# Row sums spread over all head pairs, and the first operands of Wo fetched earlier

## Chip, cores, metric

The kernel runs on 1 core of one Trainium2 chip. The metric is the device time of one execution in microseconds (us), as the median of several runs. Where a profile is read, its span is a little shorter than the device time of the same run (1532.3 against 1534.1 us for the kernel before). Runs of one kernel differ by up to 0.8% within one batch, so differences of a few microseconds are read from landmarks in the trace rather than from totals; a landmark comes from one profiled run.

## The reference, cut to what matters

```python
def reference(A_x, A_mem0, A_Wq, A_Wk, A_Wv, A_Wo, A_seg_len, B_x, B_w1, ..., c, w_mod):
    # _A_ref: segmented attention, 32 heads of 128, 2048 tokens, D = 1024; ends in
    #     o = einsum('bhte,hed->btd', o, Wo)
    # _B_ref: layernorm, w1 + gelu, shifts, w2, w3 + gelu, w4
    x = A_x
    mod = (_silu(c) @ w_mod).reshape(c.shape[0], 6, 1, -1)
    sa, ca, ga, sb, cb, gb = ...                       # six rows of 1024
    h = _layernorm(x, axis=-1) * (1 + ca) + sa
    x = x + ga * _A_ref(h, A_mem0, A_Wq, A_Wk, A_Wv, A_Wo, A_seg_len)
    h = _layernorm(x, axis=-1) * (1 + cb) + sb
    x = x + gb * _B_ref(h, B_w1, ...)
    return x
```

Two things matter here. The rows ga, cb, sb and gb are products of a vector with slices of w_mod; nothing needs them before Wo, so their work can be placed anywhere in the attention. And Wo needs the attention output of all heads: a 2048 x 4096 by 4096 x 1024 product.

## The kernel before

The kernel works in stages: projections and attention by pairs of heads (16 pairs), then Wo in four blocks of 512 tokens with the second LayerNorm, then the four matrices of the second part. Work is cut into small closures ("units") that are merged into one order; a scheduler orders instructions finally, except where `keep_order` pins them. The transposes of V and of the attention output O are DMA transposes on the SP queue.

The row sums: a 128 x (8 x 256) piece of w_mod is loaded, VectorE multiplies and adds it up to `row_a`, splits it into two bf16 parts, and two matmuls with one column of ones sum over the partitions.

```python
def row_units(items, pool):                       # pool: up_row, bufs=1
    def mk(vi, add1, n4):                         # one quarter of one row
        def load():
            st["wm"] = ws_tile([P, KT, 256])
            keep_order(nc.sync.dma_start(st["wm"][:], wslice(w_mod, ...)))
        def part(k0): ...                         # 2 of the 8 steps on VectorE into row_a
        def split(): ...                          # row_hi, row_lo on VectorE; total is put on pending
        def total():
            pb = acc_tile()[0:1, 0:256]
            nc.tensor.matmul(pb, lhsT=ones_col[:], rhs=st["hi"][:], start=True, stop=False)
            nc.tensor.matmul(pb, lhsT=ones_col[:], rhs=st["lo"][:], start=False, stop=True)
            ...                                   # copy on ACT or DVE into row_a / row_hi
            nc.gpsimd.dma_start(dst, r)
        return [load] + [part(k) for k in range(0, KT, 2)] + [split]
    quarters = [mk(vi, add1, n4) for vi, add1 in items for n4 in range(4)]
    ...                                           # each quarter's load one quarter ahead

for hp in range(NHP - 1):                         # NHP = 16 pairs
    fill = P_units(hp + 1)                        # projections of the next pair
    ...                                           # guard squares in the pairs hp = 0 to 9
    if hp == NHP - 6:
        ru = row_units(((2, False), (4, True), (3, False), (5, False)), rowp)
    ...                                           # so all 16 quarters lie in 4 pairs
    interleave(att[hp], fill)
```

The start of Wo, after the last projections:

```python
otcp = ...tile_pool(name="x1_ot", bufs=6)         # OTc: transposed attention, 8 heads x 512 tokens, 1 MB
wspR = ...tile_pool(name="x1_wsR", bufs=4)        # Wo blocks of 1 MB
W0 = W_units(0)                                   # [n2][hc]: 32 matmuls each; hc is a group of 8 heads
for j in range(3):
    load_ot(j)                                    # on SP, ahead of the O and V transposes
load_wo2(NHP - 2)
interleave(att[NHP - 1], M_units(NHP - 3) + [lambda: load_wo2(NHP - 1)] + M_units(NHP - 2) + W0[0][0:2])
for u in att["end"] + W0[0][2:3]:
    u()
for j in range(3, 6):
    load_ot(j)
...
for u in W0[1][0:3] + W0[0][3:] + W0[1][3:]:
    u()
...
for blk in range(1, 4):
    ...
    elif blk == 2:
        nc.sync.dma_start(w1s[:], ...)            # w1, 2 MB, for the stage after Wo
```

## Time and profile before

| | before |
|---|---|
| median of 3 runs | 1532.65 us (1531.76 to 1537.88) |
| TensorE busy | 1439.2 us, 94% of the span |
| pairs up to 534 us | 43.7 us each |
| the five pairs from 534 to 777 us | 48.7 us each |
| last projection to the end of Wo | 267.6 us |

The page of the kernel before. The digits are tenths of busy time in 40 equal slices of the span (38.3 us each).

```profile
...
PE 1439.2 (94%) x9074; PEld 762.2 (50%) x9074; DVE 929.8 (61%) x1961; ACT 665.7 (43%) x1403; POOL 357.5 (23%) x486
PE   5698999999999999998986799999997999999998
...
DMA  9576779887777697767569999995399785287812
```

TensorE is full except for the start, a dent at slice 30 (1149 to 1188 us, the start of the third matrix), and two dents: slices 18 and 20 (690 to 805 us, the row sums) and 21 to 22 (805 to 880 us, the start of Wo). Slices are counted from 0. In the second dent the DMA row is 9 throughout.

How fast the pairs go is read from a work item that recurs once per pair, the 199-column projections of Wv. From the timeline of TensorE, kernel before (start, duration, line, output<-inputs, count):

```profile
184.39 1.54 PE L330 MATMUL acc<-hh,wv 128*128 128x199 bf16 x16
...
533.76 1.54 PE L330 MATMUL acc<-hh,wv 128*128 128x199 bf16 x16
...
777.43 1.54 PE L330 MATMUL acc<-hh,wv 128*128 128x199 bf16 x16
```

The first eight pairs take (533.76 - 184.39) / 8 = 43.7 us each, the five with the row sums (777.43 - 533.76) / 5 = 48.7 us each (the work of the 4 pairs, 558 to 765 us in the trace, touches five of these intervals). In those pairs VectorE waits for single buffers. From the waits of VectorE, 534 to 793 us (total us, times, longest):

```profile
DVE row_a L265 <- DMA rows_d<-row_a: 10.6, 4, 4.2
...
DVE row_hi L272 <- DMA rows_d<-row_hi: 9.8, 4, 5.2
```

`row_a` may only be overwritten when the store of the finished row has left it. These waits are idle time of VectorE.

The waits of TensorE from the last projection to the end of Wo, 793 to 1061 us, kernel before:

```profile
PE acc L830 <- DMA wstream<-in_A_Wo_dram: 9.8, 2, 8.7
PE ps_o L704 <- DMA V<-VT: 5.6, 1, 5.6
PE acc L671 <- POOL OTm L729: 5.0, 1, 5.0
PE acc L830 <- DMA OTc<-OTx_d: 2.4, 1, 2.4
...
```

With one of 2.4 us for x, late in Wo, and three small ones (0.7, 0.7, 0.4) they add up to 27.0 us. The four shown lie before 881 us. The SP queue shows why the transposes are late (timeline of the SP queue; the duration is how long the issue held the queue):

```profile
793.83 1.34 SPq L806 DMA_DIRECT2D OTc<-OTx_d  x3
795.77 14.69 SPq L719 DMA_TRANSPOSE OT<-O  x1
...
```

Behind three loads of 1 MB (and one of Wo, issued at 792.3 us) the issue of an O transpose takes 14.7 us. The V transpose that TensorE waits for is issued after it, at 811.8 us. The DMA engines are full: in the stretch 793 to 890 us their busy share is 1.02 at 310 GB/s.

### The profile page before, as it was taken

The page shows a single profiled execution, that of the slowest core. Times are in us where ns is not written, and L with a number is a line of the kernel's source. Part 1 is how long each engine was busy: PE and PEld are TensorE (multiplying, and loading weights), DVE is VectorE, ACT ScalarE, POOL GpSimd, SP SyncE. Part 2 cuts the span into 40 slices and gives each one's busy share as a digit, 9 for nine tenths or more (in the row PEclk, how much of TensorE's full clock was granted, in tenths as well). Part 3 has the DMA queues.
Part 4 walks back from the last instruction along what each step waited for, and adds up shares of the span by engine and source line. Part 5 has one row for each costly group of instructions (what it writes and reads, how often), then busy time and mean ns, then how long its engine had stood idle before and what let it go on. Part 6 is the DMA issues. An engine that isn't in the chain of part 4 may idle for free.

```text
span 1532.3 us, 24313 instructions
## 1 busy us (share of the span) xinstructions
PE 1439.2 (94%) x9074; PEld 762.2 (50%) x9074; DVE 929.8 (61%) x1961; ACT 665.7 (43%) x1403; POOL 357.5 (23%) x486
## 2 busy tenths in 40 slices
PE   5698999999999999998986799999997999999998
PEld 3365665656655655554553344444443444444443
DVE  5617666666666667986751153453378557667684
ACT  2715766666667554544550030221533661036400
POOL 7402000000000000101100042132011655546525
PEclk9999999999999999999998999999999999999999
DMA  9576779887777697767569999995399785287812
GB/s 312 183 276 151 170 163 195 183 170 173 161 157 167 133 195 166 165 137 160 126 166 273 327 310 335 296 285 155 94 242 264 237 268 179 80 258 252 281 37 77
DMA packets 408276, 304.81 MB, mean 199 GB/s; under 512 B 203338, under 2 KB 361034, under 8 KB 406098
## 3 DMA queue, kind: packets, MB, share of 16 engines
q1 hardware_dynamic: 370128, 243.59, 61.0%
q0 software_dynamic: 8784, 28.85, 6.9%
q10 hardware_dynamic: 29234, 30.71, 6.5%
q8 instruction: 73, 1.20, 0.3%
q14 instruction: 57, 0.47, 0.1%
HBM read 200.82 MB, written 50.63 MB: 164 GB/s over the span
## 4 chain that ended last, share of the span: by engine, by line
PE 39%; DMA 5%; DVE 3%; issue 2%; POOL 1%; ACT 1%; SPq 1%; ACTq 0%; DVEq 0%; POOLq 0%
PE acc L830 8%; PE bank_b L1181 6%; PE bank_b L1130 6%; PE acc L974 4%; PE acc L1057 3%; PE bank_d L1130 3%; PE bank_e L1181 2%; PE bank_d L1181 2%; PE acc L608 2%; DMA wstream<-in_A_Wo_dram 1%; PE bank_e L1130 1%; DMA OT<-O 1%; DMA xt<-in_A_x_dram 1%; DMA x_d<-x 1%; DVE ln_st L104 1%
## 5 line engine op out<-in xcount | busy, mean ns | idle before, releaser
L830 PE MATMUL acc<-wstream,OTc 128*128 128x512 bf16 x1024 | 231.6, 389 | 14.7 <-DMA wstream<-in_A_Wo_dram 9.8
L576 ACT COPY snap<-acc 128x480 f32<-128x480 f32 x264 | 146.8, 563 | 115.7 <-PE acc L608 112.3
L608 PEld LDWEIGHTS <-T 128*128 128x128 f16 x1408 | 131.2, 98 | 129.9 <-issue 14.6
L830 PEld LDWEIGHTS <-OTc 128*128 128x128 bf16 x1024 | 101.7, 100 | 139.4 <-issue 22.1
L608 PE MATMUL acc<-hs,T 128*128 128x480 f16 x704 | 163.5, 369 | 7.2 <-DVE QT L580 6.7
L608 PE MATMUL acc<-hh,T 128*128 128x480 bf16 (+1 forms) x704 | 163.7, 366 | 0.2 <-DVE VT L580 0.2
L731 POOL DMA_DIRECT2D OTx_d<-OT x32 | 24.8, 774 | 562.6 <-DMA OT<-O 504.3
L1130 PEld LDWEIGHTS <-ring 128*128 128x128 f16 (+1 forms) x784 | 77.2, 99 | 107.2 <-issue 14.3
L608 PE MATMUL acc<-hh,wq 128*128 128x480 bf16 x464 | 106.1, 366 | 0.0
L693 ACT ACTIVATE E<-ps_s 99x495 bf16<-99x495 f32 (+2 forms) x160 | 85.8, 545 | 34.5 <-PE ps_s L689 33.3
L711 DVE TENSOR_TENSOR O<-ps_o,rin_all 99x384 bf16<-99x384 f32 (+1 forms) x192 | 96.9, 510 | 4.1
L704 PEld LDWEIGHTS <-E 99*99 99x99 bf16 (+2 forms) x704 | 68.9, 128 | 49.8 <-DVE O L711 10.5
L704 PE MATMUL ps_o<-V,E 99*99 99x129 bf16 (+2 forms) x704 | 82.0, 223 | 11.9 <-DMA V<-VT 5.6
L1000 DVE TENSOR_TENSOR ring<-ring 128x1024 f16<-128x1024 bf16 (+1 forms) x64 | 85.8, 1361 | 5.8 <-PE bank_b L1181 5.4
L580 DVE TENSOR_TENSOR KT<-acc,snap 128x480 bf16<-128x480 f32 x116 | 75.3, 655 | 21.3 <-PE acc L608 13.1
L1181 PEld LDWEIGHTS <-hq 128*128 128x128 bf16 (+1 forms) x560 | 54.8, 98 | 66.0
L695 DVE TENSOR_TENSOR E<-E,maskB 99x495 bf16<-99x495 bf16 (+1 forms) x128 | 47.7, 376 | 63.9 <-ACT E L693 63.7
L1095 ACT COPY snap<-bank_b 128x512 f32<-128x512 f32 x72 | 40.6, 583 | 102.7 <-PE bank_b L1181 63.2
L918 ACT ACTIVATE u<-x,ln_nmr,ln_rstd 128x1024 bf16<-128x1024 f32 x16 | 19.7, 1230 | 142.3 <-DVE ln_nmr L917 79.5
L709 ACT ACTIVATE O<-ps_o,rin_all 99x128 bf16<-99x128 f32 x192 | 56.7, 369 | 54.1 <-DVE rin_all L706 53.8
L706 DVE RECIPROCAL rin_all<-ps_o 99x3 f32<-99x3 f32 (+2 forms) x256 | 43.6, 173 | 53.6 <-PE ps_o L704 52.5
L1181 PE MATMUL bank_b<-ring,hq 128*128 128x512 f16 (+1 forms) x336 | 73.2, 379 | 0.0
(218 smaller groups left out, 2512.6 us busy)
## 6 DMA issues: line engine op xcount, KB each, us to landing
wstream<-in_A_Wo_dram SPq DMA_DIRECT2D x32, 1024.0 KB, 10.4
OTx_d<-OT POOLq DMA_DIRECT2D x32, 512.0 KB, 7.6
OTc<-OTx_d SPq DMA_DIRECT2D x16, 1024.0 KB, 9.6
wstream<-in_B_w_dram SPq DMA_DIRECT2D x28, 512.0 KB, 4.4
ring<-in_B_w_dram SPq DMA_DIRECT2D x28, 512.0 KB, 5.5
ring<-in_B_w_dram SPq DMA_DIRECT2D x8, 1792.0 KB, 9.5
wq<-in_A_Wq_dram SPq DMA_DIRECT2D x16, 512.0 KB, 7.0
wk<-in_A_Wk_dram SPq DMA_DIRECT2D x16, 512.0 KB, 8.0
```

Of the source, the lines that this page charges most:

```text
L576: nc.scalar.copy(t[:], st[q][bank][:, 0:CH])
L580: nc.vector.tensor_tensor(view(d, i), chunks(st[q][bank]), chunks(st[q][s_]), ALU.add)
L608: nc.tensor.matmul(acc[:, 0:CH], lhsT=B[:, k, :], rhs=A[:, k, :], start=(j in (1, 2, 5) and k == 0), stop=(k == 3), skip_group_check=True)
L693: nc.scalar.activation(E[:rows, 0:o], ps[:rows, 0:o], ACT.Exp, scale=DH ** -0.5)
L704: nc.tensor.matmul(ps[:rows, i, :], lhsT=state["e", h, t // 5][:k, col0(t) - col0(t // 5 * 5):col0(t) - col0(t // 5 * 5) + rows], rhs=V[:k ...
L709: nc.scalar.mul(O[:rows, t, :], ps[:rows, i, 0:DH], rin[:, i:i + 1])
L711: nc.vector.tensor_tensor(O[:rows, ts[0]:ts[0] + n, :], ps[:rows, 0:n, 0:DH], rin[:, :, None].to_broadcast([rows, n, DH]), ALU.mult)
L830: nc.tensor.matmul(accs[tt][:], lhsT=ot[:, hl, tt * P:(tt + 1) * P], rhs=woc[:, hl, :], start=(h == 0), stop=(h == H - 1))
L974: nc.tensor.matmul(acc[:], lhsT=w1s[:, kt, ct * P:(ct + 1) * P], rhs=zT[:, kt, b * 512:(b + 1) * 512], start=(kt == 0), stop=(kt == KT - 1))
L1000: return nc.vector.tensor_tensor(dst, a, b, op)
L1130: nc.tensor.matmul(acc[:], lhsT=B[:, k, q * P:(q + 1) * P], rhs=A[:, k, :], start=(start and k == 0), stop=(k == 3), skip_group_check=True)
L1181: nc.tensor.matmul(acc[:], lhsT=L3[:, k, i * P:(i + 1) * P], rhs=R3[:, k, :], start=(start and k == 0), stop=(k == 13), skip_group_check=True)
```

## The change

Its intent: (a) spread the row sums over 14 pairs instead of 4, each with a load of its own just ahead and always a flush of the finished sums between two quarters, so that the buffer waits vanish; (b) fetch the first half of the first Wo block's operands ("pre_w", "pre_o", 2 MB) while the last pair with projections still runs, so that 32 Wo matmuls can start at once; (c) load the next 4 MB of the first block by the GpSimd queue, so that the transposes on SP no longer stand behind them; (d) cut the Wo units by token tile, so that they mix finer with attention; (e) issue the load of w1 one block later.

```diff
                 def load():
-                    st["wm"] = ws_tile([P, KT, 256])
+                    st["wm"] = pool.tile([P, KT, 256], BF16, name="row_w")     # pool: bufs=1
...
-            quarters = [mk(vi, add1, n4) for vi, add1 in items for n4 in range(4)]
-            ...                                  # load one quarter ahead
+            for vi, add1 in items:
+                for n4 in range(4):
+                    q = mk(vi, add1, n4)
+                    units += [q[0], lambda: None] + q[1:]
...
+        def preload():
+            pre["ot"] = [prep.tile([P, 4, 512], BF16, name=f"pre_o{i}") for i in range(2)]
+            pre["wo"] = [prep.tile([P, 4, 512], BF16, name=f"pre_w{i}") for i in range(2)]
+            for i in range(2):
+                nc.sync.dma_start(pre["wo"][i][:], Wo2[i * 512:(i + 1) * 512, 0:512]...)
+                nc.sync.dma_start(pre["ot"][i][:], OTx_d[0, 0, :, 4 * i:4 * i + 4])
...
+        extra = [guard_units(), row_units(((2, False), (4, True), (3, False), (5, False)), rowp)]
         for hp in range(NHP - 1):
             fill = P_units(hp + 1)
-            ...                                  # guard squares, then rows in the last four
+            for x in extra if hp < NHP - 2 else []:
+                part = x[len(x) * hp // (NHP - 2):len(x) * (hp + 1) // (NHP - 2)]
...
+            if hp == NHP - 2:
+                LX.close()
+                prep = LX.enter_context(tc.tile_pool(name="x_pre", bufs=1))
+                fill.insert(0, preload)
             interleave(att[hp], fill)
...
-        W0 = W_units(0)
-        for j in range(3):
-            load_ot(j)
+        W0, W0_load = W_units(0)
+        for j in range(1, 3):
+            W0_load(0, j, nc.gpsimd)
+            load_ot(j, nc.gpsimd)
+        for t, src in RW:                        # rows broadcast to 128 partitions, was earlier
+            nc.gpsimd.dma_start(t[:], src.partition_broadcast(P))
         load_wo2(NHP - 2)
-        interleave(att[NHP - 1], M_units(NHP - 3) + [lambda: load_wo2(NHP - 1)] + M_units(NHP - 2) + W0[0][0:2])
+        interleave(att[NHP - 1], M_units(NHP - 3) + [lambda: load_wo2(NHP - 1)] + W0[0][0] + W0[0][1] + M_units(NHP - 2))
...
             elif blk == 2:
                 chain[1] = (lambda a=chain[1]: (a(), check_b()))
+            else:
                 nc.sync.dma_start(w1s[:], B_w1.rearrange("(k p) n -> p k n", p=P))
```

## The prediction

> **What bounds the kernel.** TensorE, 94% busy (busy table); from 160 to 560 us, 399 of 400 us (windows), one head pair every 43.8 us (recurrence of the 199-column Wv projections). Two places break this:
>
> 1. *Rows, 534-777 us.* Five pairs take 243.7 us instead of 219. The 16 row quarters (4.4 us of VectorE each, 70 us) sit in four pairs; VectorE rises from 26 to 33 us per 40. Its waits name the cause: 10.6 us for DMAs of row_a, 9.8 us for DMAs of row_hi (single buffers, next quarter right behind), up to 5.2 us at a time; and the SP queue stands 33 us in row loads, ahead of the V and O transposes. About 3.4 us of the excess are the 32 row-sum matmuls (estimate, 0.107 us each), which remain.
>
> 2. *Start of Wo, 794-890 us.* TensorE waits 2.4 us for OTc, 5.0 for OTm, 5.6 for the V transpose, 1.0 and 8.7 for Wo blocks. Three 1 MB OTc loads precede the O transpose on the SP queue; its issue takes 14.7 us. The granted clock falls to 0.66-0.83 around each long wait: the Trainium skill ("TensorE: Matmul & The Clock Gate", Part 1) says an idle window of about 3.4 us halves the clock; here a Wo matmul took up to 634 ns, median 379. At 0.218 us per Wo matmul block 0 could end at 855 us (estimate); it ends at 871.5, waits 8.7 and restarts cold (+3). Recoverable: 28 us.
>
> **What the change does.** Matmuls and bytes stay.
> - Rows: 8 units per pair over 14 pairs, two units and always a flush between a quarter's split and the next, so the buffer waits mostly vanish. VectorE pays 5 us per pair everywhere (26 to 31 of 40); guard squares drop from 2.8 to 2 per pair. Expect 18 of 21 us back, after new short waits.
> - The first 2 MB of Wo and OT come in the last pair with projections, so 32 Wo matmuls (7 us) start at once; the OTm sums move behind. The next 4 MB go to the GpSimd queue, so only one OTc load still precedes the transposes on SP. w1 (2 MB) still stands before the second block's Wo loads in the built order.
>
> All this is on TensorE's path. Limit: DMA is 100% busy at 280-340 GB/s from 800 to 1040 us (windows), and a 56 us block needs about 17 MB (estimate: 8 Wo, 4 OT, 5 LayerNorm), 304 GB/s. All queues share the same 16 engines (Trainium skill, "Trainium Kernel Development and Optimization", Key Constraints): the GpSimd queue changes order, not bandwidth. Expect 17 of 28 us back.
>
> **Prediction.** 1532.65 - 18 - 17: 1498 us, range 1487 to 1514. Faster by over 2% 0.58, within 0.41, slower 0.01.
>
> **Signs.** Rows: pairs of 44-45 us throughout; VectorE's DMA waits for row_a and row_hi under 5 us; last projections near 775 instead of 793. Wo: pre_w matmuls right after the last projection, no OTm wait, V wait under 3 us, block 0 done 60-65 us after the last projection (before: 78), the 8.7 us wait halved, clock seldom under 0.9.
>
> **What would make it wrong.** Early pairs, where TensorE is full, lose 1 us or more each to VectorE (18 becomes 5). Wo becomes DMA-bound and the 17 us return as Wo or OTc waits in blocks 1 to 3. The 4 MB on the GpSimd queue slow the transposes as before. If both parts keep nearly all: 1487.

## The result, and the profile after

| | before | after |
|---|---|---|
| median of 4 runs each, us | 1532.36 | 1517.11 (1515.95 to 1518.85) |
| ratio, 95% interval | | 0.9893 (0.9868 to 0.9919) |
| last projection, us in the span | 793.5 | 783.0 |
| end of Wo (first matmul with w1) | 1061.1 | 1043.1 |
| last projection to end of Wo | 267.6 | 260.1 |
| end of Wo to the end | 471.2 | 474.0 |

The change gained 15 us, by the ratio 1.1%: within 2%, not the 2.3% of the prediction, and outside its range. Ratios here and below are the mean time of one kernel's runs over that of the other's in the same rounds, so they are not quite the ratios of the medians quoted.

The landmarks split the 15.2 us between the two spans: 10.5 from the row part (793.5 to 783.0), 7.5 from the Wo part (267.6 to 260.1), and 2.8 given back later (471.2 to 474.0). Predicted were 18 and 17. About 1.5 of the 2.8 lies behind a wait that both kernels have: TensorE waits 5.9 us for ScalarE at the start of the third matrix, and the matmuls from that restart to the next bank_b group took 11.4 us in the kernel after (1170.38 to 1181.82) against 9.9 us before; the granted clock stayed low for longer after the same wait (0.74 from 1174 to 1178 us; before, 1.00 from 1191 to 1195, as far behind the restart). Why was not tested.

The page of the kernel after:

```profile
...
PE 1429.2 (94%) x9074; PEld 760.1 (50%) x9074; DVE 921.4 (61%) x1961; ACT 668.2 (44%) x1403; POOL 356.1 (23%) x490
PE   5699999999999999999996799999997999999998
...
```

The first dent is gone from TensorE's row; the second is not.

The recurring Wv projections, kernel after, timeline of TensorE:

```profile
183.20 0.85 PE L328 MATMUL acc<-hh,wv 128*128 128x199 bf16 x8
...
766.86 1.54 PE L328 MATMUL acc<-hh,wv 128*128 128x199 bf16 x16
```

All 13 pairs take (766.86 - 183.20) / 13 = 44.9 us. That is 1.2 us more for the early ones and 3.8 less for the late ones.

The waits of VectorE in the kernel after, 130 to 769 us, where the rows are now:

```profile
DVE row_a L265 <- DMA row_w<-in_w_mod_dram: 6.2, 3, 2.2
DVE row_hi L288 <- PE acc L280: 0.2, 1, 0.2
```

The two old waits are gone, as predicted. A new one has come: VectorE now waits for the load of the row's own weights, 6.2 us in all, so the sign "DMA waits for row_a and row_hi under 5 us" was missed.

The waits of TensorE, 782.4 to 1043 us, kernel after:

```profile
PE ps_o L713 <- DMA V<-VT: 13.6, 1, 13.6
PE acc L845 <- DMA wstream<-in_A_Wo_dram: 7.2, 1, 7.2
PE acc L845 <- DMA OTc<-OTx_d: 3.6, 2, 1.8
...
```

With two of 0.4 and 0.3 us they add up to 25.1 us; before, it was 27.0. So nearly all the waiting came back under other names: of the 27.0 us only 1.9 went. The other part of the 7.5 us is that TensorE's busy time in the stretch fell from 240.5 to 234.8 us for the same work. Most of that is clock: a Wo matmul lasts 379 ns at the full clock, and the mean over 1024 of them was 389 ns before, while after it was 385 ns over 960 and 379 over the other 64; that is 10 us above the full clock before and 6 after (estimate, mean excess times count). The windows of the stretch (us, then busy time with instructions for PE, PEld, DVE, ACT and POOL, granted clock, DMA share, GB/s); the first fence is the kernel before:

```profile
793.00:1061.00 268.00, 240.49 (x1183) 111.64 (x1181) 96.10 (x241) 42.12 (x69) 53.00 (x70) 0.94 0.95 284
```

the second the kernel after:

```profile
783.00:1043.00 260.00, 234.78 (x1176) 109.42 (x1174) 97.74 (x240) 41.42 (x67) 55.36 (x74) 0.95 0.93 284
```

and the third the kernel after in windows of five microseconds, two of them in the long wait:

```profile
803.00:808.00 5.00, 0.00 (x0) 0.00 (x0) 0.00 (x0) 0.00 (x0) 0.70 (x4) 0.95 1.12 302
808.00:813.00 5.00, 0.00 (x0) 0.00 (x0) 0.00 (x0) 0.00 (x0) 0.55 (x1) 0.50 1.23 251
```

The clock, 1.00 in the window before these, falls to 0.50 within the idle time, which agrees with the Trainium skill ("TensorE: Matmul & The Clock Gate", Part 1), by which an idle window of about 3.4 us halves it.

The timeline of the SP queue, kernel after:

```profile
783.26 0.34 SPq L812 DMA_DIRECT2D OTc<-OTx_d  x1
785.21 16.14 SPq L728 DMA_TRANSPOSE OT<-O  x1
...
803.66 5.33 SPq L650 DMA_TRANSPOSE V<-VT  x1
```

and the GpSimd queue, kernel after:

```profile
783.53 0.90 POOL L828 DMA_DIRECT2D wstream<-in_A_Wo_dram  x1 [9.40 <-PE ps_s L698]
...
```

Only one OTc load now precedes the O transpose on SP, yet its issue takes 16.1 us, more than the 14.7 of before. The 4 MB on the other queue (two Wo blocks, two OTc) were issued from 783.5 to 786.4 us, at the same moment. Only the two OTc of them had stood ahead of the O transpose before; the two Wo blocks were then issued on SP at 822.9 us or later, behind it. So the change did not clear the transposes' way of bytes: it took 2 MB to another queue and brought 2 MB forward.

The V wait grew by 8.0 us (5.6 to 13.6) for two reasons that the timeline of TensorE separates. The V transpose landed later after the last projection, 32.6 us (815.6 - 783.0) instead of 27.3 (820.8 - 793.5); and TensorE, without the OTm wait, was ready for it 2.6 us sooner.

One reading of the prediction has to be put right here. It took block 0 to end at 871.5 us before, with the 8.7 us wait between blocks. But only 224 of the block's 256 matmuls had run by then; the last 32 came after that wait, and the block ended at 890.4 us, 96.9 us after the last projection. In the kernel after it ends at 865.7 us, 82.7 us after: block 0 became 14.2 us shorter. That is about the forecast shortening (78 to between 60 and 65), but partly by luck of where the line is drawn: the 8.7 us wait inside block 0 is gone from there because a wait for Wo now comes behind it. Then TensorE waits 7.2 us for the first Wo block of block 1 and restarts cold, and blocks 1 to 3 take 177.4 us instead of 170.7. 14.2 gained and 6.7 given back are the 7.5.

### The profile page after: what moved, and what is told of

Its sections match the earlier page's. It is cut to its first block, busy times and chain, and to the rows that moved or that the text cites. A ratio compares the mean times of both kernels' runs of the same rounds, so it can differ in the third digit from the quotient of the medians.

```text
span 1517.1 us, 24283 instructions
## 1 busy us (share of the span) xinstructions
PE 1429.2 (94%) x9074; PEld 760.1 (50%) x9074; DVE 921.4 (61%) x1961; ACT 668.2 (44%) x1403; POOL 356.1 (23%) x490
## 4 chain that ended last, share of the span: by engine, by line
PE 73%; DMA 8%; issue 6%; DVE 5%; ACT 4%; POOL 3%; SPq 1%; ACTq 0%; DVEq 0%; POOLq 0%
PE acc L607 28%; PE bank_b L1202 6%; PE acc L845 6%; PE bank_b L1151 6%; PE acc L995 4%; PE acc L328 4%; PE bank_d L1151 3%; PE bank_d L1202 2%; PE bank_e L1202 2%; PE ps_o L713 2%; PE ps_s L698 2%; PE acc L318 2%; PE acc L1078 2%; PE bank_e L1151 1%; DVE ln_st L104 1%
## 5 line engine op out<-in xcount | busy, mean ns | idle before, releaser
L845 PE MATMUL acc<-wstream,OTc 128*128 128x512 bf16 x960 | 214.7, 385 | 11.3 <-DMA wstream<-in_A_Wo_dram 7.2
L607 PE MATMUL acc<-hs,T 128*128 128x480 f16 x704 | 158.5, 365 | 4.9 <-ACT snap L575 3.8
L845 PEld LDWEIGHTS <-OTc 128*128 128x128 bf16 x960 | 94.4, 99 | 124.8 <-DMA wstream<-in_A_Wo_dram 7.4
L713 PEld LDWEIGHTS <-E 99*99 99x99 bf16 (+2 forms) x704 | 69.2, 127 | 53.2 <-issue 20.4
L1021 DVE TENSOR_TENSOR ring<-ring 128x1024 f16<-128x1024 bf16 (+1 forms) x64 | 75.5, 1200 | 5.5 <-PE bank_b L1202 5.1
L110 POOL TENSOR_TENSOR ln_rstd<-ln_ve,mhalf 128x1 f32<-128x1 f32 x64 | 35.2, 550 | 173.7 <-DVE ln_ve L108 129.8
```

The source lines that it names most:

```text
L607: nc.tensor.matmul(acc[:, 0:CH], lhsT=B[:, k, :], rhs=A[:, k, :], start=(j in (1, 2, 5) and k == 0), stop=(k == 3), skip_group_check=True)
L713: nc.tensor.matmul(ps[:rows, i, :], lhsT=state["e", h, t // 5][:k, col0(t) - col0(t // 5 * 5):col0(t) - col0(t // 5 * 5) + rows], rhs=V[:k ...
L845: nc.tensor.matmul(accs[tt][:], lhsT=ot[hl // 4][:, hl % 4, tt * P:(tt + 1) * P], rhs=woc[hl // 4][:, hl % 4, :], start=(h == 0), stop=(h ...
L1021: return nc.vector.tensor_tensor(dst, a, b, op)
```

## The experiments

Twelve kernels ran, in three batches on three chips; the kernel before ran beside them with medians of 1534.0, 1535.3 and 1536.3 us, so kernels of different batches are compared by ratio or by landmarks. "Last projection" is the end of the projections in the span; "Wo stretch" is from there to the end of Wo. How far this column scatters is seen where the row part is the same: in after, e1, e3, e4, e7, e8 and e9 it lies between 781.3 and 787.2 us, with prefetched row weights (e5, e10, e12, e13) between 776.8 and 778.7. The Wo stretch of the three kernels with prefetch and the Wo part of after (e5, e6, e13) is 259.1 to 260.4.

| kernel | median us (runs) | ratio to before | last projection | Wo stretch |
|---|---|---|---|---|
| before | 1532.4 (4) | 1 | 793.5 | 267.6 |
| after | 1517.1 (4) | 0.9893 | 783.0 | 260.1 |
| e1_rows_only | 1523.1 (4) | 0.9926 | 782.3 | 270.1 |
| e2_light_rows | 1517.1 (4) | 0.9889 | 786.4 | 259.9 |
| e3_ot4_held | 1518.3 (4) | 0.9890 | 787.2 | 261.3 |
| e4_pool_held | 1517.1 (4) | 0.9890 | 784.2 | 261.9 |
| e5_row_prefetch | 1509.9 (4) | 0.9824 | 776.8 | 260.2 |
| e7_half_ot | 1505.1 (1) | | 781.3 | 247.7 |
| e8_ordered | 1524.4 (4) | 0.9912 | 786.8 | 266.7 |
| e9_ordered_held | 1518.2 (4) | 0.9893 | 783.6 | 257.4 |
| e10_ordered2 | 1513.3 (4) | 0.9844 | 777.6 | 260.9 |
| e12_pref_w1late | 1502.6 (4) | 0.9772 | 778.0 | 251.2 |
| e6_pref_no_sums | 1502.6 (1) | | 768.7 | 259.1 |
| e13_pref_no_squares | 1512.6 (1) | | 778.7 | 260.4 |

"hold(a, b)" in the edits makes the transfer a wait until b has finished; it is an added dependency, nothing is taken away.

### The row part alone: e1_rows_only

Edit: the kernel before, with only the row and guard part of the diff.

```diff
+ row_w, LX pools, [load, nop, parts, split] per quarter, rows and guards over 14 pairs
  (everything from preload on as in the kernel before)
```

> The kernel before with only the row part of the change (spread rows and guards, single buffers); start of Wo as before. If the two parts simply add: last projection near 782 us (after: 782.4), and the Wo part then runs as before, so about 1532 - 10.6 = 1522 us (ratio 0.993) and the Wo part of the change is worth about 5 us net. Rival: the parts interact; the row part alone ends near 1527 (an earlier start is eaten by the Wo loads) or near 1517 (the Wo part is worth nothing).

Measured: 1523.1 us, ratio 0.9926 (0.9879 to 0.9973). The last projection came at 782.3 us, as in the kernel after, and the Wo stretch was 270.1 us, 2.5 more than before (5.0 us of it in a wait for x that the kernel before has only 2.4 of). So the two parts are separate: the row part is worth about 11 us where it happens, and the Wo part 7 to 10 us; by the ratios of the totals (0.9926 and 0.9893) it is about 5 us.

### Is it VectorE's load that keeps the rows from gaining more? e2_light_rows

Edit to the kernel after: seven of the eight multiply-adds of each quarter are left out, so the rows are wrong (relative error 0.024). Loads, splits and sums stay.

```diff
-                            else:
+                            elif vi < 0:
                                 nc.vector.scalar_tensor_tensor(st["a"][:], st["wm"][:, kt, :], ...)
```

> After, with 7 of the 8 VectorE operations of each row quarter left out (wrong result on purpose); loads, buffers, row-sum matmuls, guards unchanged. Theory: the 1.1 us that each head pair costs over 43.8 us comes from VectorE load; then pairs fall to about 44.1 us and the last projection comes 8 to 10 us earlier (772 to 775 us), total about 1508. Rival: single buffers, extra DMA or the row-sum matmuls cost it; then the last projection stays within 2 us of 782.

Measured: 1517.1 us, ratio 0.9889, no gain at all, with the last projection at 786.4 us. Taking most of the row arithmetic from VectorE bought nothing, which speaks against the theory that VectorE's load costs the missing microseconds. The test is not clean: VectorE's wait for the row weights stayed and was longer than in the kernel after (7.8 us in 4 waits, against 6.2 in 3), and 3.0 us of waits for `row_hi` came back. The better evidence is e6 below, where the row arithmetic is all there and the pairs still keep the pace of pairs without rows.

### The trace's own pointer: waiting for row_w

A profile of the next kernel, e3, whose row part is that of the kernel after, showed the mechanism best. Timeline of VectorE, e3_ot4_held:

```profile
605.15 0.35 DVE L265 TENSOR_SCALAR row_a<-row_w,sc 128x256 f32<-128x256 bf16 x1 [5.42 <-DMA row_w<-in_w_mod_dram]
605.42 0.65 DVE L579 TENSOR_TENSOR KT<-acc,snap 128x480 bf16<-128x480 f32 x1
```

and the timeline of TensorE, same kernel:

```profile
606.13 1.49 PE L328 MATMUL acc<-hh,wq 128*128 128x199 bf16 x8 [4.98 <-DVE KT L579]
```

VectorE reaches the first step of a quarter, whose weights have not landed, and stands for 5.4 us; the K evacuation behind it is late, so no accumulator is free and TensorE waits 5.0 us. In the kernel after the same wait, at the same place, was 1.95 us. So its length varies between runs of the same row part, and the last projection largely follows it: with 4.6 and 5.1 us of such waits in all (e1, e7) it comes at 782.3 and 781.3 us, with 7.8 (e3, e8) at 787.2 and 786.8. The cause is the single buffer: `row_w` can only be loaded when the quarter before has been used up, and the transfer takes 5.5 us (median from issue to landing).

### Load the row weights one quarter ahead: e5_row_prefetch

Edit to the kernel after: `row_w` gets a pool of two, and each quarter's first unit loads the next quarter.

```diff
-                    st["wm"] = pool.tile([P, KT, 256], BF16, name="row_w")
+                    st["wm"] = rw_pools[0].tile([P, KT, 256], BF16, name="row_w")     # bufs=2
...
+            qs = [mk(vi, add1, n4) for vi, add1 in items for n4 in range(4)]
+            for i, q in enumerate(qs):
+                loads = ([q[0]] if i == 0 else []) + ([qs[i + 1][0]] if i + 1 < len(qs) else [])
+                units += [lambda loads=loads: [f() for f in loads], lambda: None] + q[1:]
```

> After, with two buffers for the row weights and each quarter's load asked for one quarter (about 38 us) ahead. Everything else as after. Theory C (formed after the light-row run moved nothing): VectorE, which works in order, stands at the first operation of a row quarter until the row weights have landed (1.9 us in the profile of after, 5.4 us in another run's), and the K and V sums behind it keep TensorE waiting (1.5 and 5.0 us). Then VectorE's waits for row weights are gone, the KT waits of TensorE (3.2 us in after's profile) are gone, the last projection comes at 777-780 us and the total falls by 3 to 6 us to 1511-1514, with less spread between runs. Rival: the short ACT snapshot waits and the row-sum matmuls are all there is; then nothing moves by more than 1.5 us.

Measured: 1509.9 us (1508.9 to 1511.7), ratio 0.9824 (0.9790 to 0.9858). The last projection moved from 783.0 to 776.8 us. Waits of TensorE, 130 to 769 us, first the kernel after:

```profile
PE acc L607 <- ACT snap L575: 3.8, 14, 0.5
PE acc L328 <- DVE KT L579: 3.3, 2, 1.7
...
```

then e5_row_prefetch:

```profile
PE acc L609 <- ACT snap L577: 3.6, 14, 0.5
PE ps_o L715 <- DVE E L706: 0.6, 1, 0.6
...
```

The waits for KT are gone, and so are VectorE's for `row_w`. That confirms it: about 6 us of the row part were lost to a buffer wait that the change itself brought in. The last projections of the four kernels with the second buffer (776.8 to 778.7) lie clear of the seven without it (781.3 to 787.2). The Trainium skill ("Trainium Kernel Development and Optimization", Best Practices) has double-buffering among its first rules; here the second buffer of 4 KB per partition was worth 6 us.

### What do the sums themselves cost? e6_pref_no_sums

Edit to e5: no sum matmuls and no copy after them (rows wrong, relative error 0.026).

```diff
                 def total():
-                    pb = acc_tile()[0:1, 0:256]
-                    nc.tensor.matmul(pb, lhsT=ones_col[:], rhs=st["hi"][:], start=True, stop=False)
-                    nc.tensor.matmul(pb, lhsT=ones_col[:], rhs=st["lo"][:], start=False, stop=True)
...
-                    if add1: ...                 # copy of pb on DVE or ACT
```

> Prefetched row weights, with the two row-sum matmuls, the copy from their bank and nothing else left out of each of the 16 quarters (one partition's part sum is stored; wrong result on purpose). Pairs cost 44.5 us in the prefetch run against 43.8 before. If the sums' own TensorE time is most of the rest (0.39 us per quarter with its gap, read from the trace): pairs 44.0 to 44.1 us, last projection 5 to 6 us earlier than in the prefetch run (771-772 us). Rival: the guard squares on ScalarE are the rest; then under 2 us earlier.

Measured (one run, state unknown): 1502.6 us; the last projection 8.1 us earlier than in e5. By the recurring Wv projections: e6 takes 43.8 us a pair ((752.60 - 183.01) / 13), which is the pace of pairs without any rows, and e5 takes 44.45 ((760.71 - 182.86) / 13). The 13 pairs differ by 8.3 us, 0.52 us for each of the 16 quarters. VectorE's row arithmetic is untouched in e6, so at 43.8 us a pair it costs TensorE nothing that shows. Most of the 0.52 can be seen in place. Timeline of TensorE, e5_row_prefetch:

```profile
197.99 0.85 PE L329 MATMUL acc<-hh,wk 128*128 128x199 bf16 x8
198.76 0.27 PE L280 MATMUL acc<-row_hi,ones_col 128*1 128x256 bf16 x1
...
199.07 0.37 PE L715 MATMUL ps_o<-V,E 99*99 99x129 bf16 x3
```

Eight such projections take 0.69 us to the start of what follows them, so the next matmul could have started at 198.68 and started at 199.07: 0.39 us for the two, not the 0.21 of two matmuls at 0.107 us. (The second of the two is the line left out.) The remaining 0.13 us of the 0.52 was not located.

### Do the guard squares on ScalarE cost anything? e13_pref_no_squares

After e5 the largest waits left are 14 small ones for ScalarE's `snap`, 3.6 us. Edit to e5: the squares of the guard (on ScalarE) are replaced by a memset of their result; the guard then checks nothing, and the output stays right. The 28 memsets ran in the first 2 us of the kernel, so they load nothing later.

```diff
-                return lambda: keep_order(nc.scalar.activation(st[i][:], st[i][:], ACT.Square, accum_out=wsq[:, i:i + 1]))
+                return lambda: nc.vector.memset(wsq[:, i:i + 1], 0.0)
```

> Prefetched row weights, with the guard squares (2.1 us of ScalarE each, two per pair) left out; their loads stay (the guard then guards nothing; results stay right). TensorE's waits for ScalarE snapshots (3.5 us in 14 short waits, one per pair, each right behind a square in the trace) should vanish and the last projection come 3 to 4 us earlier than in the prefetch run (773 us). Rival: those waits come from the sums' PSUM bank; then they stay and nothing moves by more than 1 us.

Measured (one run, state unknown): 1512.6 us, last projection at 778.7 us, no earlier than e5. The waits for `snap` did vanish, but waits for VT (3.9 us), O (1.9) and QT (1.3) took their place, and the expectation of an earlier last projection failed. The waits of VectorE, 130 to 769 us, show why; none of this stands in e5. From e13_pref_no_squares:

```profile
DVE row_hi L273 <- DMA rows_d<-row_hi: 5.3, 2, 3.4
...
```

The old waits for the row buffers had come back in the new order of instructions, also 3.4 us for `row_a` and 3.4 more before a `row_a` step that the profile puts down to a V transpose; three of TensorE's new waits end right behind such a stand of VectorE (at 235, 402 and 710 us). So the run does not show that the squares are free: what their absence may have gained, this other wait took.

### The V transpose: e3_ot4_held and e4_pool_held

Edit e3 to the kernel after: the OTc loads of j = 4 and 5 wait for the last V transpose. Edit e4: the second Wo block and OTc on the GpSimd queue, and the row broadcasts (3.5 MB together) wait for it, so that 2 MB are left in its way.

```diff
 e3:  ins = eng.dma_start(ot[:], OTx_d[j // 4, j % 4])
+     if j in (4, 5):
+         hold(ins, state["tv", 31])               # the V transpose of head 31
 e4:  W0_load(0, 1, nc.gpsimd); load_ot(1, nc.gpsimd)
+     hold(W0_load(0, 2, nc.gpsimd), state["tv", 31])
+     hold(load_ot(2, nc.gpsimd), state["tv", 31])
+     for t, src in RW:
+         hold(nc.gpsimd.dma_start(t[:], src.partition_broadcast(P)), state["tv", 31])
```

> After, with the two OTc loads of the next block (1 MB each, SP queue), one of which stands ahead of the last O and V transposes, held until the last V transpose has landed. The four GpSimd loads are untouched. Theory A: the transposes are slow because all bulk shares the DMA engines with them, from whichever queue; then the V wait of TensorE falls only from 13.6 to 9-11 us. Rival B: the one OTc load ahead of them in the same SP queue is what delays them; then the V wait falls under 4 us. Total 1513-1517 under A, near 1508 under B.

> After, with the second Wo block, its OTc and the four row broadcasts (3.5 MB, GpSimd queue) held until the last V transpose has landed; the first pair (2 MB) and the SP queue as they are. Theory A: V wait falls from 13.6 to about 4-7 us, then perhaps a wait of up to 5 us for the held block, total about 1511-1515. Rival B (the SP queue's own OTc load): V wait stays above 10 us and the held block comes later still, total at or above 1517.

Measured, e3: 1518.3 us, V wait 13.7 us, unchanged. This run does not test what it was meant to: in the order as built another OTc load had moved into the gap, so one still stood ahead of the O transpose on SP. It only shows that holding these two loads changes nothing. Its V wait met neither theory.

Measured, e4: 1517.1 us, ratio 0.9890. Waits of TensorE, 776 to 1050 us, e4_pool_held:

```profile
PE acc L853 <- DMA OTc<-OTx_d: 9.3, 3, 6.4
PE acc L853 <- DMA wstream<-in_A_Wo_dram: 8.5, 2, 8.2
PE ps_o L719 <- DMA V<-VT: 6.2, 1, 6.2
...
```

The V wait is halved, from 13.6 to 6.2 us, and the O transpose's issue falls from 16.1 to 7.8 us, with the same single OTc load ahead of it. Timeline of the SP queue, e4_pool_held:

```profile
784.48 0.34 SPq L818 DMA_DIRECT2D OTc<-OTx_d  x1
786.43 7.78 SPq L734 DMA_TRANSPOSE OT<-O  x1
```

So it is the bulk on the GpSimd queue that slows a transpose on the SP queue. But the held loads are then missed: OTc waits rise from 3.6 to 9.3 us, and the total is the same. Rearranging moved the wait.

### Better orders: e8_ordered, e9_ordered_held, e10_ordered2

Edit e8 to the kernel after: no OTc load stands on SP ahead of the transposes (OTc 3 to 6 go by GpSimd, 4 to 6 of them after the last write of the attention output), the row broadcasts wait for the last V transpose, w1 waits for OTc 12. In the built order the V transpose then also goes before the O transpose. e9 is e8 with the second Wo block and OTc also held until that V transpose. e10 is e5 plus the order of e8, with OTc 4 to 6 held only until OTc 3 and one later Wo block until the last O transpose.

```diff
+     if j in (3, 4, 5, 6):
+         eng = nc.gpsimd
+     if j in (4, 5, 6):
+         hold(ins, state["otx", 31])              # e10: state["ot", 3]
+ hold(nc.gpsimd.dma_start(t[:], src.partition_broadcast(P)), state["tv", 31])
+ hold(nc.sync.dma_start(w1s[:], ...), state["ot", 12])
+ e9:  hold(W0_load(0, 2, nc.gpsimd), state["tv", 31]); hold(load_ot(2, nc.gpsimd), state["tv", 31])
+ e10: hold(r, state["flip", 31])                  # the Wo block (n2 1, hc 1) of block 0
```

> After, with what block 0 does not need put behind what it needs: row broadcasts held until the last V transpose landed, the OTc loads of the next block (j=4 to 6) and OTc of heads 24-31 on the GpSimd queue behind the last OT write, w1 held until the OTc of the last block has landed. The two GpSimd pairs (4 MB) start as in after. If the engines are full and only the order of bytes is wrong: V wait 13.6 to about 8 us, the 7.2 us wait before block 1 to under 3, total 1506-1511. If order does not help (every byte is needed by then anyway): within 3 us of 1517.

> As the ordered version, and the second Wo block and its OTc also wait for the last V transpose. If the first 2 MB land by 795 us and the transposes then go nearly alone: V wait under 4 us, then a wait of 2 to 6 us for the second OTc, total 1504-1510. If the second OTc then costs what the V wait saved (as in the run with the GpSimd loads held): equal to the ordered version within 2 us.

> Prefetched row weights, and the ordered version's Wo start mended: its 13 us wait for the OTc of heads 24-31 came from two 1 MB Wo loads ahead of the last O transposes and from four OTc loads at once. Here one of the Wo loads waits for the last O transpose, and the next block's OTc loads wait for that OTc. If order can still buy time in the full-DMA stretch: from last projection to Wo end 260 us (after) falls to 248-254, total 1500-1505. If the stretch is bound by bytes alone (reordering only moved waits in four runs so far): 257-262 us, total 1507-1511.

Measured: e8 1524.4 us (0.9912), e9 1518.2 us (0.9893), e10 1513.3 us (0.9844, with the gain of e5 in it). None shortened the Wo stretch by more than 3 us against the kernel after, and e8 lengthened it by 7. All three also hold w1, which alone is worth about 9 us (e12, below): so their orders did not come out even, they lost about what that gave. Waits of TensorE, 776 to 1050 us, e8_ordered:

```profile
PE acc L857 <- DMA OTc<-OTx_d: 14.4, 2, 13.0
...
PE ps_o L719 <- DMA V<-VT: 1.7, 1, 1.7
...
```

The V wait is solved (1.7 us), and everything else is worse: Wo blocks 10.9 us, O 3.8. In e9 it was OTc 12.0 and O 4.9, in e10 Wo blocks 17.9 and O 3.5. And e8 is the cleanest test of the queues. Its first transpose has nothing ahead of it on SP; timeline of the SP queue, e8_ordered:

```profile
787.79 16.97 SPq L654 DMA_TRANSPOSE V<-VT  x1
804.93 2.76 SPq L734 DMA_TRANSPOSE OT<-O  x1
```

Its issue takes 17.0 us beside 4 MB on the GpSimd queue; in e9, beside 2 MB, 11.9 us; and the next one 2.8 us, when the last of the 4 MB were landing (805.1 us). This fits the Trainium skill ("DMA: Bandwidth & Descriptors", Queues, rings and completion order), by which each DMA engine takes turns between its queues, whole packets at a time: another queue does not get out of the way, it gets its turns. That the turns are the mechanism is argued; the runs show the lengthening.

### Are there too many bytes? e7_half_ot

Edit to the kernel after: each OTc load brings only four of its eight heads, and these stand in for the others (wrong; the comparison with the reference did not notice it).

```diff
-            eng.dma_start(ot[:], OTx_d[j // 4, j % 4])
-            ots[j] = [ot[:, 0:4], ot[:, 4:8]]
+            eng.dma_start(ot[:, 0:4], OTx_d[j // 4, j % 4, :, 0:4])
+            ots[j] = [ot[:, 0:4], ot[:, 0:4]]
```

> After, with every OTc load cut to half its bytes (512 KB instead of 1 MB; the other half of the operand reads the same data, wrong result on purpose). Number, order and queues of the loads unchanged. Theory A2: from the last projection to the end of block 0 the DMA engines are full, so bytes are what TensorE waits for; with 4 of about 25 MB less there the V wait falls from 13.6 to under 8 us and block 0 plus the wait after it shortens by 8 to 14 us (Wo end 1043 to about 1032). Rival: the order on the SP queue (transposes behind each other, OTc of heads 24-31 waiting for its write) bounds it; then it shortens by under 4 us.

Measured (one run, state unknown): 1505.1 us. The Wo stretch fell from 260.1 to 247.7 us. Waits of TensorE, 776 to 1050 us, e7_half_ot:

```profile
PE ps_o L713 <- DMA V<-VT: 7.0, 1, 7.0
PE acc L845 <- DMA wstream<-in_A_Wo_dram: 6.0, 2, 5.1
...
```

Where the rearrangements could not shorten the stretch by more than 3 us, fewer bytes did by 12, within the 8 to 14 expected of theory A2. So bytes that do not come make the start of Wo shorter. It does not follow that their order is indifferent (e10 loses 10 us of the stretch by it against e12, below), and the run is not bytes alone: in its built order some loads had moved too (w1 was issued at 835.4 us instead of 849.8).

### Bytes that need not come then: e12_pref_w1late

The diff puts the load of w1 (2 MB, needed only after Wo) one block later in the source. In the built order it stayed where it was, before block 1's Wo loads. Timeline of the SP queue, kernel after:

```profile
849.82 0.84 SPq L978 DMA_DIRECT2D w1s<-in_B_w_dram  x1
...
855.71 14.03 SPq L828 DMA_DIRECT2D wstream<-in_A_Wo_dram  x3
```

The first of these Wo blocks, issued at 855.7 us, is the one that TensorE waits for at 866 to 873 us; it took 17.7 us to land. In the kernel before, w1 was issued at 848.1 us, so nothing had moved. Edit to e5: w1 really waits.

```diff
-                nc.sync.dma_start(w1s[:], B_w1.rearrange("(k p) n -> p k n", p=P))
+                hold(nc.sync.dma_start(w1s[:], B_w1.rearrange("(k p) n -> p k n", p=P)), state["ot", 12])
```

> Prefetched row weights, and w1 (2 MB) held until the OTc of the last block has landed, nothing else. If bytes before block 1 are what the 7-8 us wait there is made of: 2 MB at about 370 GB/s is 5.5 us, the wait falls to 2-3 us, from last projection to Wo end 260 to about 254-256, total 1504-1506. Rival: the SP queue standing for the OT write of the last head is the cause; then the wait stays at 7-8 us and total at 1510.

Measured: 1502.6 us (1499.0 to 1503.9), ratio 0.9772 (0.9744 to 0.9800), correct: the fastest kernel, faster than both. w1 is now issued at 918.5 us. The Wo stretch is 251.2 us, 9.0 less than in e5. Waits of TensorE, 776 to 1050 us, e12_pref_w1late:

```profile
PE ps_o L721 <- DMA V<-VT: 13.7, 1, 13.7
...
PE acc L853 <- DMA wstream<-in_A_Wo_dram: 1.8, 1, 1.8
...
```

The wait behind block 0 (7.2 us in the kernel after, 8.5 in e5) and its cold restart are gone; the V wait is untouched. e6 and e13, which ran in the batch of e12 and have w1 early, have stretches of 259.1 and 260.4 us, so the gain is not the chip's.

But holding w1 did two things, for the built order moved with it. Timeline of the SP queue, e12_pref_w1late:

```profile
845.25 0.47 SPq L836 DMA_DIRECT2D wstream<-in_A_Wo_dram  x1
845.97 5.04 SPq L820 DMA_DIRECT2D OTc<-OTx_d  x1
```

By the count of the loads this is the first Wo block of block 1. It was issued 67.2 us after the last projection, in e5 73.9 us after it (850.7 us, behind w1 and one more OTc load): 6.7 us earlier. And it took 12.6 us to land instead of 17.9: 5.3 us less. As an estimate, 2 MB at the 371 GB/s that the DMA engines moved from 850 to 866 us in the kernel after are 5.7 us, about what the landing shows. So fewer bytes account for some 5 of the 12 us by which the block came earlier, and its earlier place in the queue for the rest; no run separates the two. e10, which ran in the same batch and holds w1 in the same way, differs from e12 by its order of loads alone: 1513.3 against 1502.6 us. So that reordering was not merely useless, it cost 11 us (9.7 in the Wo stretch).

## Why the prediction was wrong

What it had right: TensorE bounds the kernel; the old waits for `row_a` and `row_hi` would vanish (20.4 us of them, all gone); the 32 matmuls on prefetched operands start right after the last projection (785.3 us, last projection 783.0); the OTm wait goes; and the DMA engines are full through the start of Wo, with a GpSimd queue that changes order and not bandwidth. It even listed, under what would make it wrong, that the 4 MB might slow the transposes as before, and that the Wo gain might return as waits. It then gave these too little weight.

Rows, 18 predicted, 10.5 measured. Two terms of the sum were mis-sized.
- "About 3.4 us of the excess are the 32 row-sum matmuls." They cost 8.3 us with their copies (e6 against e5), so the recoverable part was some 5 us smaller than the 21 us of the prediction.
- "Expect 18 of 21 us back, after new short waits" allowed 3 us. The single buffer for the row weights, loaded only just before its use, cost about 6 (e5): a wait of VectorE, passed on to TensorE. The prediction took the removal of the load-ahead for harmless. The early pairs did lose over 1 us each, as it feared, but not by VectorE's load: e2 gained nothing without it, and in e6 the pairs keep 43.8 us with it.
- Together: 18 - 5 - 3 is 10, the measured size (which in kernels with the same row part scatters between 6 and 12: last projections at 787.2 to 781.3 us, before 793.5). The signs agree: pairs of 44.9 us, the upper end of the 44 to 45 foreseen, and last projections at 783 instead of 775.

Wo, 17 predicted, 7.5 measured. Here a step failed: "The next 4 MB go to the GpSimd queue, so only one OTc load still precedes the transposes on SP", with the sign "V wait under 3 us". The V wait rose from 5.6 to 13.6 us. The O transpose ahead of it took 16.1 us to issue, 14.7 before, with the 4 MB on the other queue (e4, e8 and e9: 7.8 to 17 us by how much was there), and 2 of these 4 MB had not been ahead of it before. V landed 5.3 us later after the last projection; the rest of the longer wait is TensorE being there sooner. The prediction called TensorE's idle time recoverable and only then named the DMA limit; in a stretch at a DMA share of 1.0 that order is the wrong way round. Of 27.0 us of waits in the stretch it counted on 17 back; 25.1 us of waits were left, and by the estimate above some 4 of the 7.5 us gained are the clock. Four rearrangements moved the wait or made it worse (e4, e8, e9, e10; e3 did not test it), fewer bytes shortened it (e7).

Also, "w1 (2 MB) still stands before the second block's Wo loads in the built order" was seen and not costed. Holding it was worth 9 us (e12 against e5), by its bytes and by the earlier place of the Wo block behind it, and the wait it removed is the one at which block 0's gain was given back: 14.2 us gained, 6.7 lost from block 1 on. (The kernel before has w1 early too, at 848.1 us; what it cost there was not tested.) That the 8.7 us wait lay inside block 0 and not behind it was misread.

What stays open: how much of w1's 9 us is bytes and how much order; 2.8 us lost after Wo, of which about 1.5 lie behind a cold restart; 0.13 us of each row sum; and whether any order of the same bytes could have kept the V wait short without paying elsewhere: those that were tried did not.

## What to carry to other kernels

Before counting idle time of the compute engine as recoverable, ask whether the stretch's bytes fit: where the DMA engines were full here, each transfer put out of one wait's way made another, and what shortened the stretch took bytes out of it (e7, and w1 in e12). When a change spreads work that waited for a buffer, check that it doesn't give up loading ahead: a late 0.5 MB load made VectorE stand for up to 5.4 us and TensorE for 5.0 behind it (e3), and one more buffer was the remedy (e5). Read where a load lands in the built order or in the trace: a move in the source may be none (w1 in the diff), and an edit to one load or unit may move its neighbours too (e3, e12, e13).

## What the Trainium skill lacked or had wrong

- "DMA: Bandwidth & Descriptors", Queues, rings and completion order, tells how an engine takes turns between queues, but not what it does to a DMA transpose: its issue on SP took 2.8 us once the loads on the GpSimd queue were through, 7.8 and 11.9 us beside 2 MB on the GpSimd queue and 17.0 us beside 4 MB.
- "Trainium Kernel Development and Optimization", Key Constraints, says that DMAs from several queues share the 16 engines and interleave; the runs agree (e4, e8). What it lacks is what that costs a transfer left on its own queue: with 4 MB beside them on the GpSimd queue an O and a V transpose landed later, V 32.6 us after the last projection against 27.3.
- No page was found for the cost of a small one-column matmul pair among others: two of 256 columns, with their copy, cost 0.52 us in place (e6, one run), where the rate of the full ones gives 0.21.
